# Key sums of the score quads moved from VectorE to GpSimd, and one tick sooner in the first chunk

## The chip, the cores and the metric

The kernel runs on one core of one Trainium2 chip. The metric is the device time of one execution in microseconds; three executions of the kernel before took 1852.26, 1851.18 and 1851.48 us, median 1851.48.

## What is computed

One Conformer block on x of 2 x 4000 x 512 in bf16: a feed-forward half step, full self-attention with one head over the 4000 tokens of each batch, a convolution module, a second feed-forward half step and a last norm. What bears on this case is the attention:

```python
B, T, D = x.shape                       # 2, 4000, 512
...
h = _layernorm(x1, axis=-1)
q = h @ w_q
k = h @ w_k
v = h @ w_v
scores = jnp.einsum('btd,bsd->bts', q, k) * scale
p = _softmax(scores, axis=-1)
attn = jnp.einsum('bts,bsd->btd', p, v) @ w_o
x2 = x1 + attn
```

## The kernel before

The tokens of each batch are cut into 8 chunks of 512 (TCB; the last has 416), 16 chunks in all (NCK). After the first feed-forward part, the attention goes over the chunks g = 0 to 15; g = 0 is the first chunk of the first batch, g = 8 that of the second. Within a chunk the loop runs over ticks kt = 0 to 31 (KT), one for each key tile of 128 tokens. Products with w_q and w_k are folded into one matrix, so the "keys" are the normed tokens themselves, transposed (hT), and the "values" are the normed tokens in rows (h).

The scores of most key tiles aren't made with plain matmuls. Four key tiles form a quad (tiles 4q+2 to 4q+5, q = 0 to 6). Two key tiles by two halves of the feature depth are treated as a 2 x 2 block matrix, and so are the two halves of the depth by two halves of the chunk's queries; seven block products then stand for eight, with sums made before and after them. A quad's key side needs four sums, each a tensor_tensor of 128 x 512 in bf16 with both inputs in SBUF: s1 = a21 + a22, s2 = s1 - a11, s4 = a12 - s2, and a21 = a11 - a21, which is written in place over the keys. They are in `k_sums`, steps 0 to 3. s1, s2 and s4 lie in one of two buffers (KF, in the region "xt"; the keys lie in the region "keys"), so that in the trace the four read xt<-keys, xt<-xt,keys, xt<-keys,xt and keys<-keys. A short form q = -1 with half the width (128 x 256) does the same for key tiles 0 and 1.

The key sums are made once a batch. `forms` calls `k_here(g, q, half)` at given ticks: half 0 makes steps 0 and 1, half 1 makes steps 2 and 3 and, two ticks later, step 4, a store of the three sums to DRAM (kfd). Later chunks read them back with `k_stream` (a load xt<-kfd), some four ticks ahead of use. In the first chunk of the first batch (g = 0) the scores are plain, and nothing there reads the sums; the quads' sums are made at ticks 4q+6 and 4q+7. The second batch's first two quads are made near the end of g = 7, its other five during g = 8, some ticks ahead of `score_quad(8, q)`, which reads them out of KF as weights. The short form is made at ticks 26 and 27 of g = 1, and 29 and 30 of g = 8.

`score_quad` issues the seven products of a quad over four ticks. Between them VectorE adds a partial sum in PSUM to another (`plus`, s<-s,xt and xt<-s,xt in the trace), and ScalarE takes the exponentials to SBUF. The exponentials are a 2 x 2 block matrix again, for the product with the values: `pair_sums` makes four sums of them on VectorE (sums<-sums in the trace), and `pv` reads those as weights of TensorE. In the first chunk of a batch VectorE also makes sums of the values (`v_here`, with operations of the same names as the key sums, work<-keys,xt among them).

The order in which instructions stand on each engine is not the order of these calls. `S.op(engine, ...)` records an operation with what it reads and writes; `Plan` then puts the recorded operations of the whole program in an order for each of the five engines (TensorE, VectorE "DVE", ScalarE "ACT", GpSimd "POOL", SyncE "SP", which issues the DMAs), by costs in a table: `cost` gives a bf16 tensor_tensor of 512 columns 150 + 0.52 x 512 = 416 ns on DVE and 450 + 512 = 962 ns on POOL. An engine works through its list in that order and waits on semaphores where an input isn't there yet; nothing is reordered when the kernel runs. GpSimd's other work is small: norm factors (a power, then a product, on 128 x 4), copies of one column, memsets, four tensor_scalar of 128 x 512 near the start and two products of 128 x 512 late in the kernel.

Since all operations are emitted in one helper, all rows of the profile have line 95, and are told apart by the names of what they write and read.

Of the kernel before, what the change touches and what calls it, by code (L numbers as in the profile page):

```python
# [559 lines left out]
class Conformer:  # L560
# [1539 lines left out]
    def k_sums(self, g, q, step):  # L2100

        S, n, b = self.S, self.k_home(g, q), g // TCB
        if step == 4:
            self.k_move(g, q, True)
            return
        if q < 0:
            a11, a12, a21, a22 = [self.hh[:, r, e] for r in range(2) for e in range(2)]
            s1, s2, s4 = [self.KF[n][:, m, 0].rearrange("p j k -> p (j k)") for m in range(3)]
            b_x = self.b_hT[0][0:2]
        else:  # L2110
            x = self.hq[:, q]
            b_x = [self.b_hT[kt // TPC][kt % TPC] for kt in self.quad_tiles(q)]
            a11, a12, a21, a22 = [x[:, :, r, e].rearrange("p u j k -> p u (j k)") for r in range(2) for e in range(2)]
            s1, s2, s4 = [self.KF[n][:, m].rearrange("p u j k -> p u (j k)") for m in range(3)]
        b1, b2, b4 = [[c] for c in self.b_KF[n]]
        out, u, v, op, rd, wr = ((s1, a21, a22, ALU.add, [], b1), (s2, s1, a11, ALU.subtract, b1, b2),
                                 (s4, a12, s2, ALU.subtract, b2, b4), (a21, a11, a21, ALU.subtract, [], b_x[1::2]))[step]
        S.op("DVE", lambda e: e.tensor_tensor(out=out, in0=u, in1=v, op=op), reads=rd + b_x, writes=wr)

    @staticmethod  # L2120
    def k_home(g, q):
# [172 lines left out]
    def forms(self, g, kt):  # L2294

        if g + 1 < NCK and 27 <= kt < 31:
            self.q_sums(g + 1, kt - 27)
        q, r = divmod(kt - 6, 4)
        if g == 0 and 0 <= q < QUADS and r < 2:
            self.k_here(0, q, r)  # L2300
        for at in {1: (26, 27), TCB: (29, 30)}.get(g, ()):
            if kt == at:
                self.k_here(g, -1, kt % 2 == g % TCB)
        q, r = divmod(kt + 2, 4)
        if r < 2:
            if g == TCB and 1 < q < QUADS:
                self.k_here(g, q, r)
            if g == TCB - 1 and q >= QUADS:
                self.k_here(g + 1, q - QUADS, r)
        q, r = divmod(kt + 3, 4)  # L2310
        if r == 0 and q and (g % TCB if q < QUADS else g and (g + 1) % TCB) and (q != QUADS or g % TCB > (g < TCB)):
            self.k_stream(*((g, q) if q < QUADS else (g + 1, q - QUADS - 1)))
        if g == 0 and kt == 30:
            self.k_stream(1, 0)
        if g:
            if kt == 2:
                self.v_stream(g, 1)
            j, r = divmod(kt + 1, 4)
            if r == 0 and 1 < j < GROUPS:
                self.v_stream(g, j)  # L2320
        if kt == KT - 1 and g + 1 < NCK:
            self.v_stream(g + 1, 0)
# [1034 lines left out]
```

## Time and profile before

| what | value |
|---|---|
| median of three runs | 1851.48 us |
| the profiled execution's own time | 1851.06 us |
| its span, first to last instruction | 1846.9 us |
| ScalarE busy | 1364.9 us (74%) |
| GpSimd busy | 144.3 us (8%), 357 instructions |
| granted TensorE clock | 1.00 in all of the stretches below |
| kfd<-xt (stores of a quad's key sums) | 16, issued 412.5 to 937.1 us |
| xt<-kfd (loads of them) | 109, issued 454.8 to 1351.2 us, median 3.2 us to landing |

The page's first part gives the busy time of each engine. "PE" is TensorE's matmuls and "PEld" its weight loads; matmuls are pipelined and their ends are modelled, so a gap shorter than a matmul's latency doesn't show as idle time. A row of a group reads: line, engine, operation, names out<-in, partitions x elements out<-in, count | busy us, mean ns of one | idle time of the engine just before them, and what ended it. A row of the timeline reads: start and length in us, engine, line, operation, names, form, count, and in brackets the idle time before it. The key sums lie between 400 and 503 us (first batch) and between 866 and 937 us (second).

### The profile page before, as it was taken

Reading aid. Unit: us, or ns where it says so; the run is one execution under the profiler, and the core shown is the slowest. Engines: PE = TensorE matmul, PEld = TensorE weight load, DVE = VectorE, ACT = ScalarE, POOL = GpSimd, SP = SyncE. Lnnn points to the kernel's source line nnn. Section 1 sums busy time; section 2 is a strip of 40 time slices with the busy share of each in tenths; the row PEclk is TensorE's granted clock in tenths of the full one; section 3 lists DMA queues with packets and bytes.
Section 4 is the critical chain, followed back from the end, with each engine's and each line's share of the span. In section 5 each row is a group of like instructions: output and inputs, shape, how many; then the busy total and the mean of one; then the engine's idle time right before and its main releaser. Section 6 shows DMA issues by size and latency. Waiting matters only on the chain.

```text
span 1846.9 us, 40836 instructions
## 1 busy us (share of the span) xinstructions
PE 1827.6 (99%) x16082; PEld 1518.8 (82%) x16168; DVE 1491.3 (81%) x3240; ACT 1364.9 (74%) x2433; POOL 144.3 (8%) x357
## 2 busy tenths in 40 slices
PE   9999999999999999999999999999999999999998
PEld 6888888866888888889878888888876888888887
DVE  8889898868766877677876777777779989889886
ACT  6887777755656877787777877887768788777775
POOL 2000000000000000000100000000011000000010
PEclk9999999999999999999999999999999999999999
DMA  7332344287645655458954444543476222211211
GB/s 200 87 91 85 83 111 100 70 245 226 173 144 143 189 153 157 125 151 178 241 146 136 123 116 117 146 122 111 124 218 171 56 69 77 73 47 48 64 44 45
DMA packets 317722, 231.09 MB, mean 125 GB/s; under 512 B 191362, under 2 KB 288325, under 8 KB 317268
## 3 DMA queue, kind: packets, MB, share of 16 engines
q1 hardware_dynamic: 316996, 228.15, 45.7%
q8 instruction: 129, 2.11, 0.5%
q14 instruction: 69, 0.57, 0.1%
q10 hardware_dynamic: 528, 0.26, 0.0%
HBM read 131.15 MB, written 56.22 MB: 101 GB/s over the span
## 4 chain that ended last, share of the span: by engine, by line
PE 95%; DVE 2%; ACT 1%; DMA 1%; issue 1%; SPq 0%; DVEq 0%; ACTq 0%
PE y L95 50%; PE s L95 45%; DVE work L95 1%; ACT work L95 0%; DVE wff L95 0%; ACT sums L95 0%; DMA work<-work 0%; DMA pqd<-wff 0%; ACT keys L95 0%; DVE xt L95 0%; DVE sums L95 0%; DVE s L95 0%; DMA xt<-kfd 0%; DVE keys L95 0%; ACT xt L95 0%
## 5 line engine op out<-in xcount | busy, mean ns | idle before, releaser
L95 ACT ACTIVATE sums<-s 128x512 bf16<-128x512 f32 (+4 forms) x498 | 291.3, 586 | 145.9 <-PE s L95 143.0
L95 ACT ACTIVATE keys<-s 128x512 bf16<-128x512 f32 (+3 forms) x275 | 156.9, 574 | 132.7 <-PE s L95 101.6
L95 DVE TENSOR_TENSOR sums<-sums 128x512 bf16<-128x512 bf16 (+3 forms) x528 | 201.3, 399 | 54.6 <-ACT sums L95 42.2
L95 PE MATMUL y<-work,keys 128*128 128x256 bf16 x1920 | 244.4, 273 | 0.0
L95 PE MATMUL s<-sums 128*128 128x256 bf16 (+1 forms) x1428 | 212.6, 272 | 0.1
L95 PE MATMUL y<-sums,keys 128*128 128x256 bf16 (+1 forms) x1440 | 210.6, 270 | 0.0
L95 PE MATMUL y<-wff,keys 128*128 128x256 bf16 (+2 forms) x1590 | 209.4, 276 | 0.1
L95 ACT ACTIVATE work<-xt,work 128x512 bf16<-128x512 bf16 x260 | 199.5, 784 | 9.5 <-DVE work L95 7.8
L95 PEld LDWEIGHTS y<-work,keys 128*128 128x128 bf16 x1920 | 187.8, 98 | 22.4
L95 PE MATMUL y<-work,wff 128*128 128x256 bf16 (+3 forms) x1324 | 197.2, 272 | 0.1
L95 DVE TENSOR_TENSOR keys<-keys 128x1024 bf16<-128x1024 bf16 (+2 forms) x264 | 170.7, 660 | 22.9 <-ACT keys L95 20.2
L95 PE MATMUL s<-work,keys 128*128 128x256 bf16 (+4 forms) x1329 | 184.6, 275 | 1.0
L95 PEld LDWEIGHTS y<-wff,keys 128*128 128x128 bf16 (+1 forms) x1592 | 151.4, 98 | 30.2 <-issue 3.4
L95 DVE BATCH_NORM_STATS2 work<-xt 128x6 f32<-128x512 bf16 x251 | 164.3, 681 | 2.4 <-DMA xt<-in_x_dram 1.7
L95 PEld LDWEIGHTS s<-sums 128*128 128x128 bf16 x1428 | 139.0, 98 | 22.5 <-DVE s L95 0.4
L95 PEld LDWEIGHTS y<-sums,keys 128*128 128x128 bf16 x1440 | 138.1, 98 | 21.3 <-issue 2.9
L95 POOL TENSOR_TENSOR work<-work 128x4 f32<-128x4 f32 (+3 forms) x108 | 91.2, 845 | 764.8 <-DVE work L95 741.8
L95 PE MATMUL s<-xt,keys 128*128 128x256 bf16 (+1 forms) x924 | 142.3, 270 | 1.2 <-DVE s L95 1.1
L95 PEld LDWEIGHTS y<-work,wff 128*128 128x128 bf16 x1324 | 127.3, 98 | 17.6 <-DVE wff L95 0.4
L95 PE MATMUL y<-sums,xt 128*128 128x256 bf16 (+1 forms) x960 | 140.7, 270 | 0.3 <-DVE sums L95 0.3
L95 PEld LDWEIGHTS s<-work,keys 128*128 128x128 bf16 (+1 forms) x1348 | 107.7, 97 | 34.9 <-ACT sums L95 2.2
L95 PE MATMUL s<-xt 128*128 128x256 bf16 (+1 forms) x893 | 131.4, 270 | 1.3 <-DMA xt<-kfd 0.9
(163 smaller groups left out, 3343.9 us busy)
## 6 DMA issues: line engine op xcount, KB each, us to landing
xt<-kfd SPq DMA_DIRECT2D x98, 384.0 KB, 3.2
xt<-v12d SPq DMA_DIRECT2D x105, 256.0 KB, 3.1
xd<-xt SPq DMA_DIRECT2D x28, 512.0 KB, 2.7
xt<-xd SPq DMA_DIRECT2D x28, 512.0 KB, 3.8
out_dram<-xt SPq DMA_DIRECT2D x14, 512.0 KB, 2.9
xt<-in_x_dram SPq DMA_DIRECT2D x13, 512.0 KB, 4.4
dcvd<-wff SPq DMA_DIRECT2D x48, 128.0 KB, 2.9
keys<-dcvd SPq DMA_DIRECT2D x12, 512.0 KB, 3.7
```

The lines of the kernel that those rows point to most:

```text
L95: return getattr(eng, self.name)(*self.args, **self.kw)
```

## The change

`k_sums` gives its four sums to GpSimd instead of VectorE, in both batches: 14 quads and two short forms, 64 operations. In the first chunk (g = 0) `forms` calls `k_here` one tick sooner, at ticks 4q+5 and 4q+6. The store of a quad in that chunk is recorded a tick sooner with it. The planner is as it was; it is given GpSimd's cost for these operations, and makes a new order from them.

```diff
@@ k_sums
         out, u, v, op, rd, wr = ((s1, a21, a22, ALU.add, [], b1), (s2, s1, a11, ALU.subtract, b1, b2),
                                  (s4, a12, s2, ALU.subtract, b2, b4), (a21, a11, a21, ALU.subtract, [], b_x[1::2]))[step]
-        S.op("DVE", lambda e: e.tensor_tensor(out=out, in0=u, in1=v, op=op), reads=rd + b_x, writes=wr)
+        S.op("POOL", lambda e: e.tensor_tensor(out=out, in0=u, in1=v, op=op), reads=rd + b_x, writes=wr)
@@ forms
-        q, r = divmod(kt - 6, 4)
+        q, r = divmod(kt - 5, 4)
         if g == 0 and 0 <= q < QUADS and r < 2:
             self.k_here(0, q, r)
```

In the new order the 64 operations stand on GpSimd between its memsets of the keys' ones columns (first batch) and its norm steps and column copies (second batch), each of a quad's sums waiting for GpSimd's own one before it where it reads its result, and the in-place one for TensorE's last reading of those keys. On TensorE and ScalarE the instructions of the two stretches stand in a somewhat different order; on SP some stores of key sums change places with neighbouring loads and stores.

## Prediction

> **What bounds the kernel now.** I read the page's busy shares and chain of waits first, then the busy times of stretches, then TensorE's waits, and last the groups by form.
>
> ```profile
> span 1846.9 us, 40836 instructions
> ...
> PE 1827.6 (99%) x16082; PEld 1518.8 (82%) x16168; DVE 1491.3 (81%) x3240; ACT 1364.9 (74%) x2433; POOL 144.3 (8%) x357
> ...
> PE 95%; DVE 2%; ACT 1%; DMA 1%; issue 1%; SPq 0%; DVEq 0%; ACTq 0%
> ```
>
> TensorE sets the end: it is busy 99% of the span and 95% of the chain. The change issues no matmul more or less, so it can only alter how long TensorE waits. The key sums stand in two stretches, one for each batch:
>
> ```profile
> core 0: us, PE busy (x) PEld busy (x) DVE busy (x) ACT busy (x) POOL busy (x), PEclk, DMA share, GB/s
> 412.00:460.00 48.00, 47.74 (x316) 29.73 (x320) 38.91 (x104) 25.16 (x43) 2.26 (x16) 1.00 0.77 236
> 876.00:940.00 64.00, 62.86 (x568) 51.97 (x570) 54.68 (x130) 49.67 (x91) 4.63 (x15) 1.00 0.95 232
> ```
>
> TensorE is idle for 0.3 us in the first and 1.1 us in the second, at a full granted clock; VectorE is 81% and 85% busy, GpSimd nearly free. From 860 to 945 TensorE's recorded waits are these two; from 385 to 510 there is none.
>
> ```profile
> PE s L95 <- DVE sums L95: 0.5, 1, 0.5
> PE s L95 <- DVE wff L95: 0.2, 1, 0.2
> ```
>
> So there are 0.7 us that a freer VectorE can win for certain, and a good deal that a later VectorE can lose.
>
> **The change part by part.** *Off VectorE.* A quad has four sums; each batch has seven quads (128x512) and one short form (128x256, q = -1).
>
> ```profile
> L95 DVE TENSOR_TENSOR xt<-xt,keys 128x512 bf16<-128x512 bf16 x14 | 5.9, 420 | 0.3
> L95 DVE TENSOR_TENSOR xt<-xt,keys 128x256 bf16<-128x256 bf16 x2 | 0.6, 287 | 0.0
> ```
>
> The second sum alone shows 14 + 2; four of each make 56 x 0.420 + 8 x 0.287 = 25.8 us that leave VectorE. What TensorE gets of it is between 0 and the 0.3 + 1.1 us of idle time above; I take the 0.7 us of the waits.
>
> *Onto GpSimd.* The trace has two GpSimd sums of this form:
>
> ```profile
> L95 POOL TENSOR_SCALAR keys<-keys,work 128x512 bf16<-128x512 bf16 x4 | 7.3, 1830 | 0.4
> ...
> L95 POOL TENSOR_TENSOR wff<-wff 128x512 bf16<-128x512 bf16 x2 | 2.3, 1156 | 9.5 <-ACT wff L95 9.5
> ```
>
> So 56 x 1.156 = 65 us on an engine that has room. The four sums of a quad hang together, about 4.6 us instead of 1.7. Is that soon enough? The quad with the shortest lead among the wide ones:
>
> ```profile
> 924.57 0.42 DVE L95 TENSOR_TENSOR xt<-keys 128x512 bf16<-128x512 bf16 x1
> ...
> 930.01 0.33 PEld L95 LDWEIGHTS s<-xt 128*128 128x128 bf16 x4 [0.28 <-ACT wff L95]
> ```
>
> Its first sum is ready 5.0 us before the first weight load that reads it. Begun at the same moment on GpSimd it is ready at 925.7, and the margin is 4.3 us. The first batch's sums go to DRAM and are read back a chunk later; the earlier tick adds a tick more. I cost lateness at 0 here; what hides it is this lead.
>
> *The cover that is lost: both engines read SBUF at once.* In the first 33 us GpSimd ran four wide operations beside VectorE. The first, third and fourth, each with the VectorE sum that came behind it, and two usual means:
>
> ```profile
> 24.75 1.90 POOL L95 TENSOR_SCALAR keys<-keys,work 128x512 bf16<-128x512 bf16 x1
> 25.23 1.06 DVE L95 TENSOR_TENSOR work<-work,wff 128x1024 bf16<-128x1024 bf16 x1
> 28.54 2.04 POOL L95 TENSOR_SCALAR keys<-keys,work 128x512 bf16<-128x512 bf16 x1
> 29.19 1.06 DVE L95 TENSOR_TENSOR keys<-keys 128x1024 bf16<-128x1024 bf16 x1
> 30.68 1.67 POOL L95 TENSOR_SCALAR keys<-keys,work 128x512 bf16<-128x512 bf16 x1
> 30.95 0.80 DVE L95 TENSOR_TENSOR sums<-sums,wff 128x512 bf16<-128x512 bf16 x1
> ...
> L95 DVE TENSOR_TENSOR sums<-sums 128x512 bf16<-128x512 bf16 x408 | 165.5, 422 | 49.1 <-ACT sums L95 38.8 <-DVE sums L95 0.5
> L95 DVE TENSOR_TENSOR keys<-keys 128x1024 bf16<-128x1024 bf16 x240 | 161.0, 686 | 22.3 <-ACT keys L95 20.2
> ```
>
> Each VectorE sum of two SBUF inputs lost 1.06 - 0.69 = 0.37 or 0.80 - 0.42 = 0.38 us. One that reads PSUM lost nothing, though it stands in the time of the second operation:
>
> ```profile
> 27.54 0.69 DVE L95 TENSOR_TENSOR s<-s,sums 128x512 f32<-128x512 f32 x1
> ...
> L95 DVE TENSOR_TENSOR s<-s,sums 128x512 f32<-128x512 f32 x115 | 79.8, 694 | 16.0 <-PE s L95 14.4 <-ACT keys L95 0.6
> ```
>
> Those four read one wide input; a key sum reads two. One pair in the trace has a two-input GpSimd sum:
>
> ```profile
> 1380.38 1.16 POOL L95 TENSOR_TENSOR wff<-wff 128x512 bf16<-128x512 bf16 x1
> 1380.68 1.05 DVE L95 TENSOR_SCALAR work<-xt,work 128x512 bf16<-128x512 bf16 x1
> ...
> L95 DVE TENSOR_SCALAR work<-xt,work 128x512 bf16<-128x512 bf16 x18 | 7.2, 437 | 0.1
> ```
>
> Without this one the mean is (18 x 0.437 - 1.05) / 17 = 0.40, so it lost 0.65 us and ran only from about 0.95 us after GpSimd began. The block of a key sum is thus between 2 x 0.38 = 0.76 and 0.95 us; I take 0.8, nearer to the rows with VectorE sums.
>
> [...]
>
> How often does a key sum meet such an operation?
>
> ```profile
> L95 DVE TENSOR_TENSOR sums<-sums 128x512 bf16<-128x512 bf16 x28 | 11.3, 421 | 3.8 <-ACT sums L95 3.5
> ...
> L95 DVE TENSOR_TENSOR sums<-sums 128x512 bf16<-128x512 bf16 x28 | 11.2, 421 | 1.9 <-ACT sums L95 1.1
> L95 DVE TENSOR_TENSOR s<-s,xt 128x512 f32<-128x512 f32 x8 | 5.6, 699 | 1.9 <-PE s L95 1.7 <-ACT xt L95 0.3
> L95 DVE TENSOR_TENSOR xt<-s,xt 128x512 f32<-128x512 f32 x7 | 4.8, 683 | 0.9 <-PE s L95 0.9
> ```
>
> The first row is from 412 to 458, the rest from 866 to 938. The pair sums (sums<-sums) alone fill 11.3 / 46 = 25% and 11.2 / 72 = 16% of these; all of VectorE's work, without some 8 and 12 us of key sums, about 65% and 67%. Between these bounds I take 0.5 for the first batch, where most of the rest are SBUF sums too (the values' forms), and 0.35 for the second, where much of it reads PSUM. That is 32 x 0.5 = 16 and 32 x 0.35 = 11 blocks, 27 x 0.8 = 22 us: VectorE gets back nearly all that it gave away, but as lumps of 0.8 us that the hand-made order did not count on.
>
> How much of a lump reaches TensorE?
>
> ```profile
> 443.84 0.75 DVE L95 TENSOR_TENSOR sums<-sums 128x512 bf16<-128x512 bf16 x2
> ...
> 444.98 0.32 PEld L95 LDWEIGHTS s<-sums,keys 128*128 128x128 bf16 x3
> ...
> 914.84 0.70 DVE L95 TENSOR_TENSOR s<-s,xt 128x512 f32<-128x512 f32 x1 [0.28 <-ACT xt L95]
> ...
> 915.60 0.33 PEld L95 LDWEIGHTS s<-xt,keys 128*128 128x128 bf16 x4 [0.37 <-DVE s L95]
> ```
>
> In the first batch a pair sum is ready 0.39 us before TensorE reads it: of a lump 0.8 - 0.39 = 0.4 is left, and half the lumps fall ahead of such a place: 16 x 0.5 x 0.4 = 3.2 us. In the second, the score quads' additions (s<-s,xt) are awaited with no slack: of 11 lumps I let two thirds reach one, 7 x 0.8 = 5.6 us. Bounds: none arrives (0), or 27 x 0.95 with no slack anywhere, less a quarter (19 us).
>
> *What queues behind.* On GpSimd the norms' small steps wait behind a key sum, up to 1.2 us, and VectorE waits for those in turn:
>
> ```profile
> L95 POOL TENSOR_TENSOR work<-work 128x4 f32<-128x4 f32 x2 | 1.4, 725 | 0.2
> ...
> L95 DVE SCALAR_TENSOR_TENSOR work<-work 128x4 f32<-128x4 f32 x55 | 8.6, 157 | 3.6 <-POOL work L95 3.1
> ```
>
> Two such steps stand in the second stretch; at most 2 x 1.2 = 2.4 us, at least 0; VectorE's waits for GpSimd are 3.1 us in 55 cases, so I take 0. GpSimd's memsets of the keys' ones columns now also stand behind in-place sums that wait for TensorE's scores, and the other way about; on SP each store of a quad (16 of them) waits for the third sum, some 2 us later after its start than before, with the loads and transposes of keys queued behind it. No wait of TensorE in either stretch is for a DMA, so both are taken at 0, with 0 to 3 us for the range. The planner also reorders some matmuls around both stretches; their number is the same: 0, with 1 us either way.
>
> *Sum.* -0.7 + 3.2 + 5.6 = +8.1 us on the profiled execution's 1851.06 us (span 1846.9 and 4.2 around it): 1859.2. The median, 1851.48, is 0.4 above that execution, so 1859.6; I say 1859.5.
>
> **The rivals.** *Absorbed* (not slower): the lumps fall where VectorE is idle anyway, 19% and 15% of the stretches, and the 25.8 us of relief pays for them. For it: relief and lumps are about equal in sum. Against it: the zero slack at 915.60. It decides if fewer than about one lump in six reaches TensorE; time -0.7 to +3, about 1852.
>
> *Relief wins* (faster): VectorE's pair sums come sooner, at 924 for one, where TensorE waits 0.5 us for them. It needs that GpSimd's reads block next to nothing; the price is bounded by the idle 0.3 + 1.1 us plus gaps that the modelled matmul ends hide, estimated at as much again: 1848.5 to 1851.
>
> *GpSimd late* (slower too): blocked behind VectorE's sums, 0.42 us each, a quad's four sums take 4 x (1.16 + 0.42) = 6.3 us or more. If they also start 3 us later, the 4.3 us margin is gone and TensorE waits at the quad's first product, some 1.5 us at each of seven quads of the second batch: +10, 1862. Against it: the margins of about 4 us.
>
> **How the numbers follow.** Lumps as reckoned, 0.56; GpSimd late, 0.10; absorbed, 0.25; relief wins, 0.09. 0.2% is 3.7 us, about what a measurement of this kernel can tell from no change. Slower by more: 0.66 (the first two, their lower tails given up to absorbed). Within: absorbed and the greater part of the relief, which can hardly pass 3 us: 0.28. Faster by more: 0.06. The range runs from 1850, nearly all relief and no lump, to 1870, +19 of the upper bound; the likeliest case alone holds 1855 to 1867.
>
> **What would show it.** In the changed profile: key sums on GpSimd at 1.2 to 1.6 us each; VectorE's sums<-sums in 412 to 460 and 876 to 940 with a mean of 0.5 us or more instead of 0.42, single ones at 1.2; s<-s,xt still at 0.70; TensorE's idle time there up from 1.4 to about 8 us, ended by VectorE's sums and s. If the mean of sums<-sums stays at 0.42, the block is wrong and the time is that of relief. If it rises and TensorE's waits do not, the slack was larger: absorbed. If TensorE waits for GpSimd's xt, it is the late chain. A loss outside these two stretches would be none of these.

## The result and the profile after

| kernel | median | runs | ratio to before |
|---|---|---|---|
| before, beside it | 1852.26 us | 1851.18 to 1853.21 | |
| changed | 1874.41 us | 1869.23 to 1875.29 | 1.0112, 95% interval 1.0100 to 1.0123 |

The changed kernel is slower by 22.2 us, where 8 were forecast; the range ended at 1870. The profiled execution took 1875.29 us, with a span 24.1 us longer than before. Its page gives the span, the busy times and the chain of waits by engine:

```profile
span 1871.0 us, 40955 instructions
...
PE 1842.8 (98%) x16168; PEld 1523.1 (81%) x16168; DVE 1503.7 (80%) x3176; ACT 1366.1 (73%) x2433; POOL 217.9 (12%) x421
...
PE 93%; DVE 3%; DMA 1%; ACT 1%; issue 1%; POOL 0%; SPq 0%; DVEq 0%; POOLq 0%
```

VectorE gave away 64 sums (3240 instructions before, 3176 now) and is busy for longer than before, 1503.7 against 1491.3 us. TensorE's part of the chain falls from 95% to 93%. What is missing there stands in the two stretches of the prediction:

```profile
core 0: us, PE busy (x) PEld busy (x) DVE busy (x) ACT busy (x) POOL busy (x), PEclk, DMA share, GB/s
412.00:460.00 48.00, 41.00 (x234) 22.85 (x232) 38.25 (x64) 19.32 (x34) 22.17 (x35) 0.89 0.67 204
876.00:940.00 64.00, 61.29 (x568) 51.24 (x567) 51.53 (x100) 46.96 (x90) 33.63 (x39) 0.97 0.98 216
```

TensorE was busy 47.74 of the first 48 us before and is busy 41.00 now. The column behind POOL is new to the argument: the granted clock, 1.00 in both rows before, is 0.89 and 0.97. Two things were lost, then: time in which TensorE waits, and time in which it runs slower. TensorE's waits in the whole run, in us: total, times, longest:

```profile
PE s L95 <- DVE sums L95: 6.2, 3, 3.2
PE y L95 <- DVE xt L95: 4.0, 2, 2.0
PE s L95 <- DVE s L95: 3.0, 4, 1.4
...
PE s L95 <- DMA xt<-kfd: 1.1, 1, 1.1
...
PE y L95 <- DVE keys L95: 0.9, 1, 0.9
```

What is new is for VectorE (the DMA's wait was 0.9 us before); none is for GpSimd. The groups by form, first of the whole run, then in 412 to 474 us:

```profile
L95 POOL TENSOR_TENSOR xt<-keys 128x512 bf16<-128x512 bf16 x14 | 17.5, 1250 | 13.9 <-PE y L95 10.0 <-PE s L95 3.8
...
L95 POOL TENSOR_TENSOR keys<-keys 128x512 bf16<-128x512 bf16 x14 | 16.6, 1185 | 24.2 <-PE s L95 23.5
...
L95 DVE TENSOR_TENSOR sums<-sums 128x512 bf16<-128x512 bf16 x408 | 184.5, 468 | 56.7 <-ACT sums L95 46.4 <-DVE sums L95 0.5 <-PE y L95 0.2
...
L95 DVE TENSOR_TENSOR sums<-sums 128x512 bf16<-128x512 bf16 x28 | 23.4, 856 | 8.7 <-ACT sums L95 8.4
L95 DVE SCALAR_TENSOR_TENSOR work<-work 128x3 f32<-128x3 f32 x1 | 1.2, 1172 | 0.3 <-POOL work L95 0.3
```

A key sum takes 1.19 to 1.25 us on GpSimd. VectorE's pair sums, 421 ns before, take 856 ns on the mean in this stretch. In both stretches together 42 VectorE operations beside a key sum are over 150 ns longer than the median of their form, 32.4 us in all (25 with 20.4 us in the first stretch, 17 with 12.0 us in the second). They are called held up from here on.

How four such lumps become one wait of TensorE is seen in the timeline (start and length in us; idle time before in brackets):

```profile
446.42 1.15 POOL L95 TENSOR_TENSOR keys<-keys 128x512 bf16<-128x512 bf16 x1 [1.88 <-PE s L95]
446.46 1.40 DVE L95 TENSOR_TENSOR xt<-work 128x512 bf16<-128x512 bf16 x1
...
447.53 1.33 POOL L95 TENSOR_TENSOR xt<-keys 128x512 bf16<-128x512 bf16 x1
...
447.78 1.37 DVE L95 TENSOR_TENSOR xt<-keys 128x512 bf16<-128x512 bf16 x1
...
448.94 1.21 POOL L95 TENSOR_TENSOR xt<-xt,keys 128x512 bf16<-128x512 bf16 x1
449.18 1.25 DVE L95 TENSOR_TENSOR xt<-keys,xt 128x512 bf16<-128x512 bf16 x1
450.23 1.21 POOL L95 TENSOR_TENSOR xt<-keys,xt 128x512 bf16<-128x512 bf16 x1
...
450.47 1.26 DVE L95 TENSOR_TENSOR keys<-keys 128x512 bf16<-128x512 bf16 x1
...
450.49 0.39 PE L95 MATMUL y<-sums,xt 128*128 128x256 bf16 x2 [1.98 <-DVE xt L95]
...
451.78 1.04 PE L95 MATMUL y<-sums,keys 128*128 128x256 bf16 x4 [0.90 <-DVE keys L95]
```

GpSimd's four sums stand in a row, and each of VectorE's four (sums of the values, 0.42 us when alone) ends soon after the GpSimd sum that it meets: 0.83 to 0.98 us are lost four times over, and TensorE stands idle for 1.98 and then 0.90 us. The same holds for all: each of the 42 ends 0.02 to 0.29 us after a GpSimd sum's end, 33 of them 0.28 or 0.29. What an operation loses is thus nearly what is left of the GpSimd sum when it comes (1.11, 1.08, 0.97 and 0.97 us were left in these rows, 0.98, 0.95, 0.83 and 0.83 are lost), up to 1.0 us and 0.77 on the mean.

Right behind that the clock falls. It does so on a fixed grid: all half-clock periods of this trace begin a whole number of times 3.413 us apart (the four later ones in the two stretches 5, 10, 134 and 151 times behind the first). The rows are grid steps before a fall, each followed by the fall:

```profile
430.52:433.93 3.41, 0.61 (x5) 0.29 (x3) 3.34 (x4) 2.70 (x5) 3.40 (x11) 1.00 0.90 277
433.93:437.34 3.41, 3.00 (x11) 1.53 (x12) 2.18 (x4) 0.72 (x2) 1.32 (x3) 0.50 1.05 405
447.59:451.00 3.41, 1.31 (x7) 0.31 (x4) 3.34 (x4) 1.19 (x2) 3.25 (x3) 1.00 0.55 109
451.00:457.83 6.83, 6.05 (x28) 4.18 (x29) 6.73 (x16) 0.00 (x0) 0.44 (x1) 0.50 0.62 210
...
887.87:891.29 3.42, 1.46 (x15) 1.23 (x16) 3.35 (x7) 0.74 (x2) 1.68 (x2) 1.00 0.92 259
891.29:894.70 3.41, 3.41 (x18) 2.36 (x16) 3.27 (x5) 1.99 (x4) 2.36 (x2) 0.50 0.32 69
```

Five falls (the other two at 468.04 and 949.32) hold 20.5 us at half clock. At half the clock half of that is lost, 10.2 us, if TensorE had work throughout. TensorE's idle stretches over 60 ns sum to 22.5 us, against 9.6 before: 12.9 us more. 12.9 + 10.2 = 23.1 of the 24.1 us.

A step need not be idle for a fall: the five steps ahead of the falls hold 0.61 to 1.46 us of matmuls.

### The profile page after: what moved, and what is told of

It is laid out like the page before. It is cut to its first block, busy times and chain, and to the rows that moved or that the text cites. A ratio compares the mean times of both kernels' runs of the same rounds, so it can differ in the third digit from the quotient of the medians.

```text
span 1871.0 us, 40955 instructions
## 1 busy us (share of the span) xinstructions
PE 1842.8 (98%) x16168; PEld 1523.1 (81%) x16168; DVE 1503.7 (80%) x3176; ACT 1366.1 (73%) x2433; POOL 217.9 (12%) x421
## 4 chain that ended last, share of the span: by engine, by line
PE 93%; DVE 3%; DMA 1%; ACT 1%; issue 1%; POOL 0%; SPq 0%; DVEq 0%; POOLq 0%
PE y L95 49%; PE s L95 44%; DVE sums L95 1%; DVE work L95 1%; DVE xt L95 1%; ACT sums L95 1%; DVE wff L95 0%; DMA pqd<-wff 0%; ACT work L95 0%; DMA wff<-keysd 0%; POOL xt L95 0%; DVE s L95 0%; DMA work<-work 0%; DMA xt<-kfd 0%; DMA dcvd<-wff 0%
## 5 line engine op out<-in xcount | busy, mean ns | idle before, releaser
L95 DVE TENSOR_TENSOR sums<-sums 128x512 bf16<-128x512 bf16 (+3 forms) x528 | 224.1, 442 | 62.9 <-ACT sums L95 50.5
L95 PE MATMUL y<-wff,keys 128*128 128x256 bf16 (+3 forms) x1592 | 209.8, 276 | 0.0
L95 ACT ACTIVATE work<-xt,work 128x512 bf16<-128x512 bf16 x260 | 199.5, 785 | 12.1 <-DVE work L95 10.4
L95 PEld LDWEIGHTS y<-work,keys 128*128 128x128 bf16 x1920 | 187.7, 98 | 22.5
L95 PE MATMUL s<-work,keys 128*128 128x256 bf16 (+4 forms) x1348 | 190.5, 278 | 0.5 <-DVE xt L95 0.4
L95 DVE TENSOR_TENSOR keys<-keys 128x1024 bf16<-128x1024 bf16 (+2 forms) x248 | 165.2, 681 | 22.5 <-ACT keys L95 20.3
L95 PEld LDWEIGHTS s<-sums 128*128 128x128 bf16 x1428 | 139.0, 98 | 22.5 <-DVE s L95 0.4
L95 DVE TENSOR_TENSOR s<-s,xt 128x512 f32<-128x512 f32 (+1 forms) x119 | 81.5, 685 | 65.7 <-PE s L95 54.8
```

Of the source, the lines that this page charges most:

```text
L95: return getattr(eng, self.name)(*self.args, **self.kw)
```

## The experiments

The table holds what every reading below uses. "Idle" is the sum of TensorE's idle stretches over 60 ns, less the 9.6 us of before; "half clock" is the time at 0.5 in the profiled execution, without that at the very end, which the kernel before has too; "held up" counts VectorE's operations as above.

| kernel | median, us | ratio, 95% interval | span less 1846.9 | idle | half clock | held up |
|---|---|---|---|---|---|---|
| changed | 1874.41 | 1.0100 to 1.0123 | +24.1 | +12.9 | 20.5 | 42, 32.4 us |
| e1_engine_only | 1869.15 | 1.0073 to 1.0106 | +20.4 | +11.8 | 13.7 | 39, 30.0 |
| e2_sooner_only | 1852.81 | 0.9994 to 1.0013 | +0.3 | +1.6 | 0 | 0 |
| e3_no_reads | 1850.51 | 0.9983 to 1.0003 | -1.3 | -0.7 | 0 | 0 |
| e4_one_read | 1854.67 | 1.0005 to 1.0025 | +1.2 | +1.4 | 0 | 31, 10.9 |
| e5_kept_warm | 1869.46 | 1.0078 to 1.0112 | +18.2 | +5.9 | 6.8 | 43, 32.4 |
| e6_halves | 1864.16 | 1.0045 to 1.0078 | +13.8 | +9.7 | 3.4 | 65, 25.8 |
| e7_beside | 1882.25 | 1.0143 to 1.0177 | +30.5 | +22.5 | 13.7 | 46, 38.2 |
| e8_second_only | 1858.09 | 1.0021 to 1.0046 | +6.4 | +4.5 | 3.4 | 17, 11.5 |
| e9_changed_again | 1870.96 | 1.0090 to 1.0117 | +20.8 | +13.6 | 13.7 | 43, 32.8 |
| e10_warm_more | 1866.16 | 1.0066 to 1.0094 | +16.2 | +6.5 | 0 | 43, 33.4 |
| e11_quarters | 1860.55 | 1.0036 to 1.0063 | +12.9 | +6.7 | 10.2 | 53, 12.5 |
| e12_spread | 1869.14 | 1.0080 to 1.0116 | +16.2 | +12.1 | 6.8 | 39, 29.0 |
| e13_every_other | 1855.24 | 1.0010 to 1.0030 | +3.9 | +1.5 | 0 | 19, 15.0 |

The kernel before took 1851.09 to 1852.26 us (medians) beside these. In the traces of e3, e4, e5, e10 and e13 the weight loads of TensorE and all instructions of VectorE and ScalarE stand in the changed kernel's order, one by one, and in e7's they stand in the order of before. In e1, e2, e6, e8, e11 and e12 the planner made another order, so these change more than one thing. One fall each of e5, e6 and e11 lies near 1416 us, far outside the two stretches; it is all of e6's half clock. Idle time plus half of the half-clock time comes within 1.3 us of the longer span in nine rows; in e1, e6 and e13 1.8 to 2.4 us are open, and in e5 and e10 the added matmuls come on top (below).

**The two edits apart.** e1 keeps the old tick, e2 the old engine:

```diff
-        q, r = divmod(kt - 5, 4)          # e1, in the changed kernel
+        q, r = divmod(kt - 6, 4)
...
-        q, r = divmod(kt - 6, 4)          # e2, in the kernel before
+        q, r = divmod(kt - 5, 4)
```

> The key sums move to GpSimd, but start at their old tick. Theory (a key sum that reads two SBUF tiles blocks VectorE's own two-tile operations by some 0.75 us; TensorE idles behind them, and where an idle stretch is long the granted clock falls to one half for 3.4 us or more): nearly the whole loss of the changed kernel, 1866 to 1878 us, with half-clock periods in the two stretches where the sums are made. Rival (the earlier tick does it, by a new order): 1850 to 1856 us.

> The key sums stay on VectorE; only the tick of the first chunk is one sooner. Theory: no second reader of SBUF, so 1850 to 1855 us, no half-clock period and TensorE idle by about the 1.4 us of the before kernel in the stretch of the sums. Rival (the earlier tick does it): 1866 us or more.

The engine alone costs 17 us, the tick alone nothing that can be told from 0. The four executions of e1 (1868.19 to 1871.56 us) lie among the ten of the changed kernel (1866.49 to 1875.29, listed below), so with the engine moved the tick isn't seen to matter either.

**Without the reading.** GpSimd writes, but reads nothing; the planner is given the old cost, so that the order stays.

```diff
-        S.op("POOL", lambda e: e.tensor_tensor(out=out, in0=u, in1=v, op=op), reads=rd + b_x, writes=wr)
+        S.op("POOL", lambda e: e.memset(out, 0.25), reads=rd + b_x, writes=wr)
```

> As the changed kernel, but each key sum is left out and GpSimd fills its tile with a constant instead, at the same place and with the same waits; every other engine has the changed kernel's order. Theory: GpSimd reads nothing, so VectorE's sums<-sums keep 0.42 us, the clock stays full, and the time is 1849 to 1854 us. Rival (the new order that the change makes costs the time, whoever does the sums): 1868 us or more. Rival (the result comes late from GpSimd): not told apart here, since a fill is shorter than a sum.

The group of pair sums over the whole run, and the first stretch:

```profile
L95 DVE TENSOR_TENSOR sums<-sums 128x512 bf16<-128x512 bf16 x408 | 165.8, 422 | 55.3 <-ACT sums L95 45.3 <-DVE sums L95 0.5
```

```profile
412.00:474.00 62.00, 61.74 (x441) 41.42 (x445) 41.71 (x107) 32.90 (x57) 13.31 (x40) 1.00 0.76 219
```

With the changed kernel's order on all other engines the loss is gone, the mean back at 422 ns and TensorE busy 61.74 of 62 us. So the new order costs nothing. The run also shows what the relief of VectorE is worth when nothing spoils it: 0.7 us of TensorE's idle time in the whole run, 0.4 of it in the second stretch (0.93 before, 0.54 here), and no time that can be told from 0.

Beside fills, which only write (0.53 us each), the pair sums thus keep their 422 ns. Beside a sum of two tiles the later operation can lose nearly the whole of it: in the changed kernel VectorE lost 0.98 us of a GpSimd sum's 1.15 at 446.46 us. The next run has GpSimd read one tile.

**Half the reading.**

```diff
-        S.op("POOL", lambda e: e.tensor_tensor(out=out, in0=u, in1=v, op=op), reads=rd + b_x, writes=wr)
+        S.op("POOL", lambda e: e.tensor_scalar(out, u, 0.5, None, ALU.mult), reads=rd + b_x, writes=wr)
```

> As the changed kernel, but GpSimd makes each key sum from one of its two tiles alone (halved), the other is left out; order and waits are the changed kernel's. GpSimd's one-tile operation of this size took 1.43 us in the trace of before and held a VectorE operation up by some 0.38 us, against 1.2 us and 0.75 us for a key sum of two tiles. Theory (the time for which VectorE is blocked counts): the operations that meet one lose up to 0.4 us, few or no half-clock periods, 1851 to 1862 us. Rival (GpSimd is late, and what waits for it costs the time): its operations are longer still, so 1874 us or more.

```profile
L95 POOL TENSOR_SCALAR xt<-keys 128x512 bf16<-128x512 bf16 x28 | 43.7, 1561 | 16.2 <-PE s L95 7.1 <-PE y L95 6.4 <-DMA kfd<-xt 2.0
...
L95 DVE TENSOR_TENSOR sums<-sums 128x512 bf16<-128x512 bf16 x408 | 169.6, 431 | 52.0 <-ACT sums L95 41.9 <-DVE sums L95 0.5
```

GpSimd's operations are longer, 1.56 instead of 1.25 us, and what waits for them gets it later. (The four one-input operations in the trace of before took 1.67 to 2.04 us, not the 1.43 of the expectation.) Yet the loss is 2.5 us (1854.67 - 1852.15) instead of 22: a held-up operation loses 0.35 us (10.9 / 31) instead of 0.77. *GpSimd late* falls with this. The timeline shows how the longer operation holds up less:

```profile
424.16 1.49 POOL L95 TENSOR_SCALAR xt<-xt 128x512 bf16<-128x512 bf16 x1
424.18 0.87 DVE L95 TENSOR_TENSOR xt<-keys,xt 128x512 bf16<-128x512 bf16 x1
```

VectorE's operation is through 0.60 us before GpSimd's is, and so are most of the 31 (26 by 0.60 to 0.66 us). Beside a two-input sum it ends 0.28 us after it.

**The reading without the move.** VectorE keeps its key sums; GpSimd makes sums that nobody needs.

```diff
+        if q >= 0:
+            x, b = (self.vst[:, 0:512], self.vst[:, 512:1024], self.vs2), [self.b_vst, self.b_vs2]
+            S.op("POOL", lambda e: e.tensor_tensor(out=x[0], in0=x[1], in1=x[2], op=ALU.subtract), reads=b, writes=b)
```

> The kernel before, with its key sums on VectorE as they were; beside each wide one GpSimd makes a 128x512 sum of two tiles in a scratch tile that nobody waits for. So no result comes late and nothing is moved off VectorE. The extra sums are extra work in full. Theory (the shared reading alone does it): VectorE's sums<-sums are held up as in the changed kernel, TensorE waits and its clock falls, 1863 to 1885 us. Rivals (the result is late from GpSimd, or the new order costs it): nobody waits for these sums, so 1850 to 1856 us.

```profile
L95 POOL TENSOR_TENSOR wff<-wff 128x512 bf16<-128x512 bf16 x58 | 70.5, 1216 | 18.4 <-ACT wff L95 9.5 <-PE y L95 5.7
...
L95 DVE TENSOR_TENSOR sums<-sums 128x512 bf16<-128x512 bf16 x408 | 177.1, 450 | 46.0 <-ACT sums L95 35.8 <-DVE sums L95 0.5
```

56 of the 58 rows are the added sums. They cost 30 us, more than the change: VectorE has its own key sums as well, and 38.2 us of hold-ups. The order on the other engines is that of before. With e3 this settles the first half of the cause, in both directions: no reading, no loss; reading alone, the loss.

**One batch.**

```diff
-        S.op("POOL", lambda e: e.tensor_tensor(out=out, in0=u, in1=v, op=op), reads=rd + b_x, writes=wr)
+        S.op("POOL" if g >= TCB else "DVE", lambda e: e.tensor_tensor(out=out, in0=u, in1=v, op=op), reads=rd + b_x, writes=wr)
```

> As the changed kernel, but only the second batch's key sums (the stretch near 866 to 955 us) are on GpSimd; the first batch's stay on VectorE. In the changed kernel some 7.7 us of its loss came in that stretch, 15.9 us in the first batch's. Theory: the two stretches add up, so 1857 to 1863 us, with falls of the clock in the second stretch alone. Rival (the first batch's order, moved on, is what costs in the second): 1850 to 1855 us.

6.2 us slower than the kernel before beside it, with idle time and the one fall in the second stretch alone. So the second batch's loss stands without the first's. The first batch's alone was not run; that the two add up fits, and isn't shown.

**The clock.** Matmuls that wait for nothing are set ahead of the waiting ones (their places counted in TensorE's order); they multiply the identity by itself.

```diff
+    nth, FILL = {}, {3688: 48, 3768: 30, 3836: 30, 8134: 32}     # e10 has 7664: 22 too
...
+        self.nth[e] = self.nth.get(e, -1) + 1
+        if e == "PE":
+            for _ in range(self.FILL.get(self.nth[e], 0)):
+                self.eng[e].matmul(fn.args[0][:, 0:128], self.ident, self.ident, start=False, stop=False, skip_group_check=True)
         req = self._required(reads, writes)
         self._emit_waits(e, req)
```

> The changed kernel with 140 short matmuls more (128x128), which wait for nothing: 48, 30, 30 and 32 of them stand right before the four matmuls that waited 3.21, 1.98, 2.01 and 2.09 us in the changed kernel's trace, so that TensorE has work in most of each stall. They add to the sums in PSUM, so those change. Nothing else is in another place. Theory (the granted clock falls to one half because TensorE stood idle for too much of one 3.41 us stretch, and that costs as much again as the waiting does): the waits for VectorE stay, 4 of the 5 falls of the clock (6 of its 7 periods of one half or so) are gone, and the time is 6 to 9 us below the changed kernel's, 1865 to 1869 us. Rival (the waits are the whole loss, the clock's fall is bookkeeping or is hidden): no gain, 1872 to 1878 us, or a loss by the added matmuls.

> The changed kernel once more, beside the two next ones. 1869 to 1876 us. If the falls of the clock depend on how much of a stall lies in one stretch of a fixed 3.41 us grid, single executions differ by whole falls, 1.7 us each, so they scatter by several us where the kernel before scatters by some 2.

> As the run with 140 added matmuls, with 22 more ahead of the matmul at 890.53 us that waited 1.43 us, before the last fall of the clock that was left in the two stretches. They add to sums in PSUM, so those change. Theory (idle TensorE makes the clock fall): no period of half clock in the two stretches, 6 to 9 us below the changed kernel in the same comparison, 1866 to 1868 us. Rival (the waits are the whole loss): as the changed kernel, or later by the added matmuls.

In e5 the falls at the four filled stalls are gone, the one at 884 us (891 in the changed kernel) stays, and another comes at 1420 us. Its 1869.46 us lie between the two forecasts, just above the theory's 1869. e10 fills the stall at 884 us as well. The stretches of e10:

```profile
412.00:474.00 62.00, 58.42 (x461) 38.01 (x460) 52.95 (x91) 27.43 (x47) 28.54 (x40) 1.00 0.66 199
866.00:954.00 88.00, 83.97 (x826) 71.27 (x825) 73.85 (x143) 65.95 (x126) 43.47 (x51) 1.00 0.90 212
```

The clock is full in both, and as many operations are held up as before (43). Against the changed kernel beside it e10 gains 4.8 us (1870.96 - 1866.16), less than the 6 to 9 expected. The span fits without any clock: 6.5 us of idle time, and the 162 added matmuls, whose five rows take 2.84, 1.84, 1.84, 1.39 and 1.95 us, 9.9 in all, make 16.4 of +16.2. The waiting alone thus costs some 15 us (1866.16 - 1851.09).

Single executions of the changed kernel, from both comparisons, say the same without any edit. Mean granted clock and time:

| clock | us |
|---|---|
| 0.999 | 1866.49 |
| 0.997 | 1869.23, 1869.88, 1870.72 |
| 0.996 | 1870.96 |
| 0.995 | 1871.80, 1874.00, 1874.41, 1875.18 |
| 0.994 | 1875.29 |

The execution with the highest clock takes what e10 takes. e10's own five executions lie within 1.7 us (1865.62 to 1867.34) at 0.999 or 1.000. The clock costs the changed kernel from next to nothing to 9 us, some 5 in the median of these ten, and some 7 in the median of the first comparison (22.2 less the 15 of waiting); the gain of e10 was overestimated because the trace it was reckoned from is of the execution with the lowest clock of all ten.

**Smaller pieces.**

```diff
-        S.op("POOL", lambda e: e.tensor_tensor(out=out, in0=u, in1=v, op=op), reads=rd + b_x, writes=wr)
+        for k in range(2) if q >= 0 else (slice(None),):
+            S.op("POOL", lambda e, o=out[:, k], a=u[:, k], b=v[:, k]: e.tensor_tensor(out=o, in0=a, in1=b, op=op), reads=rd + b_x, writes=wr)
```

> As the changed kernel, but each wide key sum is made in two halves of 128x256: twice as many GpSimd sums, each some 0.7 us, so GpSimd is busy for a little longer in all. Theory (a VectorE operation is held up by what is left of one GpSimd sum): twice the chances to be held up, but at most 0.4 to 0.5 us each; single stalls of TensorE are shorter, the clock falls more seldom or not at all, and the time is between the two kernels, 1857 to 1870 us. Rival (the results come late from GpSimd): they come later still, 1874 us or more.

The quarters (e11) cut each half at column 128 again.

> As the changed kernel, with each wide key sum in four pieces of 128x128. GpSimd issues four times as many sums and is busy longer than with halves. Theory (what counts is how long one sum holds VectorE up): single hold-ups under 0.3 us, TensorE idle some 14 us in all against 22.5 in the changed kernel and 19.3 with halves, no fall of the clock, 1854 to 1861 us, below the 1864 us of the halves. Rival (the time is set by GpSimd's busy time, or by results that come late): 1864 us or more.

One group of each, halves first:

```profile
L95 POOL TENSOR_TENSOR xt<-keys 128x256 bf16<-128x256 bf16 x30 | 23.7, 789 | 22.0 <-PE s L95 10.4 <-PE y L95 7.7 <-DMA kfd<-xt 2.9
```

```profile
L95 POOL TENSOR_TENSOR xt<-keys 128x128 bf16<-128x128 bf16 x56 | 27.1, 484 | 12.3 <-PE s L95 5.8 <-PE y L95 2.3 <-DMA kfd<-xt 1.8
```

GpSimd's time for this sum of the 14 quads, 17.5 us in the changed kernel, rises to 22.1 us (28 of the 30 in the first row, the other two are the short form's) and 27.1 us, and the kernel gets faster: 1.0112, 1.0061, 1.0049 of before. The intervals of halves and quarters overlap. Single hold-ups fall from 0.77 to 0.40 and 0.24 us on the mean. Neither size reaches the kernel before. Three points of the quarters missed: single hold-ups reach 0.50 us, TensorE is idle for 16.3 us (9.6 + 6.7) and not 14, and their profiled execution had three falls of the clock, two of them in the stretches. Since the planner's order differs in both runs, the gain isn't shown to come from the size of the pieces alone.

The halves show that a stall as such is not enough for a fall. The largest, 1.86 us, lies wholly in one step of the grid (laid by the later fall of that trace):

```profile
429.23:432.64 3.41, 1.55 (x11) 0.83 (x10) 3.05 (x7) 2.24 (x4) 3.32 (x13) 1.00 0.83 237
432.64:436.06 3.42, 3.42 (x22) 1.92 (x20) 0.82 (x2) 2.15 (x5) 3.22 (x8) 1.00 1.07 409
```

1.55 us of matmuls, and no fall; 1.46 us in the changed kernel, and a fall; the same 1.55 us in the quarters' step from 453.71 us, and a fall. In the two stretches of all these traces, each step with 1.9 us of idle time or more was followed by a fall from full clock, none with less than 1.7 was, and between these it went either way (falls behind 1.72, 1.85 and 1.86 us, none behind 1.72, 1.74 and 1.86). Near 1416 us, outside them, e5, e6 and e11 have a fall behind 1.64, 1.58 and 1.64 us. So the idle time that shows isn't quite what decides, and the bound stays open.

**Lumps in a row.** Why did so much more reach TensorE in the first stretch than reckoned? e12 tries to pull a quad's sums apart there, e13 takes every second one away:

```diff
         if g == 0 and 0 <= q < QUADS:                      # e12
+            self.k_sums(0, q, r)                           # one a tick; the last quad's fourth with its third
...
+        if step % 2:                                       # e13
+            S.op("POOL", lambda e: e.memset(out, 0.25), reads=rd + b_x, writes=wr)
```

> As the changed kernel, but in the first chunk a quad's four sums are recorded one a tick (at ticks 4q+5 to 4q+8) instead of two and two in neighbouring ticks; the second batch is as in the changed kernel. The planner still decides where they stand, so they come apart only in part. Theory (hold-ups that follow on each other add up to one long wait, since the slack of TensorE is used once): about as many operations are held up, but TensorE's idle time in the first stretch falls from 9 us to 2 to 6, with at most two falls of the clock there: 1857 to 1867 us. Rival (every hold-up costs its share, however they lie): as the changed kernel, 1868 us or more.

> As the changed kernel, with the first and third sum of each quad on GpSimd as they are, and the second and fourth left out: GpSimd fills their tiles with a constant, 0.53 us each, at the same place. The order on every engine is the changed kernel's. So half the reading sums are left, and between two of them VectorE has some 0.5 us. Theory (hold-ups in a row add up to one long wait): clearly less than half the loss, 1852 to 1859 us, without a fall of the clock. Rival (every hold-up costs its share): half the loss, 1860 to 1863 us.

e12 landed where its rival would: 1869.14 us, 8.3 us of idle time in the first stretch instead of 9.0. But it doesn't tell the two apart, for the sums did not come apart: ahead of its longest stall, 2.72 us at 448.62, six of them stand in a row on GpSimd (440.01 to 447.82). e13 does tell: 15.0 of 32.4 us of hold-ups are left, 46%, but 3.1 of 13.8 us of added idle time in the two stretches, 23%, and 3.8 us (1855.24 - 1851.45) of the time lost. Hold-ups did not cost their share: those that followed on others cost more than those that stood apart. (The table's 1.5 and 12.9 are of the whole run, and outside the stretches e13's trace has 1.6 us less idle time than that of before.)

## Why the prediction was wrong in size

*Right:* the direction and the mechanism. The key sums take 1.19 to 1.25 us (1.2 to 1.6 forecast); those that meet a two-input operation of VectorE hold it up, by 0.77 us on the mean (0.8 forecast); s<-s,xt, which reads PSUM, stays at 0.70 us; TensorE waits for VectorE's sums, s and values, not for GpSimd. The relief of 0.7 us has the size of what e3 shows, which can't be told from 0. What was costed at nothing is nothing, or little: the tick (e2), the new order (e3), and lateness and GpSimd's small steps behind the wide ones, which are at most the 2.5 us of e4, whose wide ones are longer still.

*Right by luck in part:* the 0.8 us of a hold-up. It was twice the 0.38 us beside a one-input operation. But beside two-input sums all 42 held-up operations end 0.02 to 0.29 us behind the sum's end, and 0.77 is the mean of what they lose to sums of 1.2 us. The second stretch's 5.6 us is luck too. Measured are 4.8 (5.75 - 0.93), but from 17 hold-ups of 12.0 us in all, of which 0.4 arrives, and not from 11 lumps of 8.8 us, of which two thirds arrive.

*Wrong, first: "16 x 0.5 x 0.4 = 3.2 us" for the first batch.* Both factors were too small. The number of blocks was the share of VectorE's time that two-input sums fill, 0.5 and 0.35; measured were 25 and 17 of 32, 0.78 and 0.53 (and two more beside the first batch's short sums, at 515 and 519 us). A GpSimd sum of 1.2 us has room for two or three VectorE operations of 0.42 us, and the first two-input one among them is held up, so the chance is higher than the share of time; this reason fits the counts, and wasn't tested. And 0.4 us of slack was taken off each lump, and half of the lumps dropped, as if they came singly. A quad's four sums stand in a row on GpSimd, so the slack is spent once and the rest arrives: of the four lumps at 446 to 452 us, 3.6 us in all, TensorE waits for 1.98 and 0.90. The first stretch has 9.0 us more of idle time, not 3.2.

*Wrong, second: the clock.* The sum was made "at a full granted clock" because the rows of before had 1.00, as if that were a constant. It is a result: TensorE's longest wait there was 0.5 us, and e10, with the stalls filled, has 1.00 again. In the two stretches each step of 3.41 us at full clock with 1.9 us of idle time or more was followed by one step, once two, at half clock, and by estimate (half of 3.41) TensorE pays up to 1.7 us in each. That was no term, no bound and no rival. It makes some 7 us of the 22.2 measured (22.2 less the 15 us that e10 shows for waiting alone), and half of the 20.5 us at half clock, 10, in the profiled execution.

The bound of 19 us that set the range's end had neither: 27 lumps instead of 42, and no clock. Of the rivals, *absorbed* and *relief wins* fall with the result itself, *GpSimd late* with e4. Why e10's waiting costs 15 us where the changed kernel's trace has 13.8 us of it in the two stretches isn't settled. With its added matmuls counted as waiting, e10's trace has 15.7 us there, so the waits are longer at full clock; that half clock gives VectorE time to catch up would fit, and was only argued.

Of the versions that make the sums, none beats the kernel before. e3, which leaves the sums out, shows why there is little to win: with VectorE relieved of all 64, the time is 0.9983 to 1.0003 of before.

## What to carry to other kernels

Before work with two SBUF inputs goes from VectorE to GpSimd, look at what VectorE runs meanwhile, not at how idle GpSimd is: if those are two-input sums too, the moved time comes back as hold-ups (25.8 us left VectorE here, and 32.4 us of hold-ups came). Count on one hold-up for each GpSimd sum that a two-input operation can start beside, nearly as long as what is left of the sum (0.77 us on the mean for sums of 1.2 us here), and let a row of them spend the slack once (2.9 us of four in a row, 3.6 us in all, reached TensorE here). Where TensorE is the bound at a full clock, price a new stall of some 2 us at its own length and up to 1.7 us more, an estimate from the 3.41 us at 0.5 that followed here wherever one step of the grid held 1.9 us or more of idle time.

## What the runs showed of the hardware that was not expected

- The granted clock fell to 0.5 for one step of 3.41 us, once for two, behind each step of the two stretches with 1.9 us or more of idle time, on a grid that does not start with the kernel: one of its steps begins at 433.93 us in the changed kernel's trace and at 432.64 in that of e6. Ten executions of one program, at mean clocks of 0.999 to 0.994, differ by 8.8 us, the slower the lower the clock; with five of its stalls filled (e10) five executions differ by 1.7. The kernel before varies by 2 to 4 us in one comparison.
- A small operation was held up like a wide one: work<-work of 128x3 elements, 0.16 us alone, took 1.17 us beside a key sum and ended 0.02 us after it. Both its tiles lie in SBUF; none of the nine additions s<-s,xt and xt<-s,xt of 128x512, of which one input lies in PSUM, that started within a key sum was held up (0.68 to 0.72 us each, medians 0.69 and 0.70).
- GpSimd's longer operations held VectorE up for less when they had one input: 0.35 us on the mean beside one-input operations of 1.56 us, 0.77 us beside two-input ones of 1.2 us. Beside a two-input sum the held-up operation ends 0.28 us after it in most cases, beside a one-input one 0.60 us before it ends.
